# One load for the second row block of a weight matrix, in a kernel whose weight loads are issued from one queue

## The chip, the core and the metric

The kernel runs on one core of a Trainium2 chip. The metric is the device time in microseconds of one execution. Results of a pair come from the same chip in alternation. The profile shows one execution of each kernel; its span, from the first to the last instruction, is some 1.3 us shorter than that execution's time.

## The reference

Two branches work on the same input `x` of 2048 tokens by 640 features (bf16) and are mixed by a gate for each token:

```python
g = sigmoid((x * gate_w).sum(-1, keepdims=True))
a = state_space(x)                       # a linear recurrence over the 2048 tokens, 640 complex states
b = gelu(x @ w1 + b1) @ w2 + b2          # w1: 640 x 1728, w2: 1728 x 640
out = g * a + (1 - g) * b
```

What matters is the beginning: `x @ w1`. Its contraction runs over 640 features, five row blocks of 128 rows of `w1`.

## The kernel before

The kernel is written as operations with priorities. A list scheduler in the program, fed with guessed durations, fixes their order on each engine at build time. All loads that matter here are issued by the SP engine, in order of `prio` (cut, with `KN` = 2 filled in):

```python
WSPLIT = {1: 6, 3: 6}                    # row blocks of W1 whose first 1024 columns come in two loads

def w1load(k, eng, prio):
    edges = [0] + ([WSPLIT[k] * 128] if k in WSPLIT else []) + [FW]          # FW = 1024
    for i, (f0, f1) in enumerate(zip(edges, edges[1:])):
        load(f"w1_{k}{i}", eng, f"l_w1{k}{i}", W1sb[:, k, f0:f1],
             B_w1[k * 128:(k + 1) * 128, f0:f1], [("w1", k, i)], prio=prio + 0.1 * i, lat=2.6)

def w1tok(k, jf):                        # which of the loads a matmul has to wait for
    return ("w1", k, int(jf >= WSPLIT.get(k, NW)))

load("xna", "sp", ...)                   # 512 tokens, first 256 features
w1load(0, "sp", 1)
w1load(1, "sp", 1.3)
xtrans(0, range(2, 3), 1.6, 0.8)         # transpose while loading: input features 256 to 383
w1load(2, "sp", 2)
xtrans(0, range(3, 4), 3, 0.8)
w1load(3, "sp", 4)
xtrans(0, range(4, 5), 4.5, 0.8)
w1load(4, "sp", 5)
... # the other columns of W1, the state-space matrices, the rest
```

TensorE starts with matmuls on constants, which need no data, then transposes the first 256 features of `x` (`f_xt`, line 427, eight instructions), VectorE copies the results out of PSUM (line 433, four copies), and the first stage of the product follows (`m1_first`, line 640). It goes through seven of the eight output banks for row block 0 before it touches row block 1 (the eighth follows just before row block 1 needs it), so that loads can arrive while it works:

```python
steps = [(0, 0, 0), (0, 1, 0), (0, 0, 1), (0, 1, 1)] + [(k, jf, None) for k, jf in seq if k or jf > 1]
# ... one matmul each: 4 of 256 columns and 5 of 512 with row block 0,
#     then row block 1 (its last two steps are (0, 7), (1, 7)), then 2, 3, 4
```

The matmul that first reads row block 1 is thus TensorE's tenth in this stage. I call it **the tenth matmul** below.

Of the kernel before, what the change touches and what calls it, by code (L numbers as in the profile page):

```python
# [184 lines left out]
def bass_gated_mix__ssm_conv_s5__dense_activation_gelu__prompt_kernel(  # L185
# [40 lines left out]
    with ExitStack() as es:  # L226
# [127 lines left out]
            load_T(f"xT{q}_{ks[0]}", f"l_xT{q}_{ks[0]}", [(xT[q][:, ks[0]:ks[-1] + 1, :], x2[q * 512:(q + 1) * 512, ks[0] * 128:(ks[-1] + 1) * 128])],  # L354
                   [("xT", q, k) for k in ks], prio, dur)

        WSPLIT = {1: 6, 3: 6}

        def w1load(k, eng, prio):
            edges = [0] + ([WSPLIT[k] * 128] if k in WSPLIT else []) + [FW]  # L360
            for i, (f0, f1) in enumerate(zip(edges, edges[1:])):
                load(f"w1_{k}{i}", eng, f"l_w1{k}{i}", W1sb[:, k, f0:f1], B_w1[k * 128:(k + 1) * 128, f0:f1], [("w1", k, i)], prio=prio + 0.1 * i, lat=2.6)

        def w1tok(k, jf):
            return ("w1", k, int(jf >= WSPLIT.get(k, NW)))

# [727 lines left out]
```

## Time and profile before

| kernel before | value |
|---|---|
| time, median of the 3 runs given | 212.67 us (212.47 to 213.09) |
| span of the profiled run | 212.1 us |
| TensorE busy | 98% of the span |
| first matmul of `m1_first` | 5.25 us |
| the tenth matmul | 7.16 us |
| last matmul done | 210.15 us |

How to read it: TensorE is the bound, and a load can only matter where TensorE waits for it. So the profile has to be asked what TensorE waits for, and how long before its first use each load has landed (in the trace the semaphore of each of these loads has 16 increments, and the last is taken as the landing).

### The profile page before, as it was taken

What the parts mean: (1) busy time and instruction counts of PE and PEld (TensorE: products, weight loads), DVE (VectorE), ACT (ScalarE), POOL (GpSimd) and SP (SyncE); (2) the same over time, 40 slices, a digit from 0 to 9 for tenths busy, and PEclk for the clock granted to TensorE, in tenths of its full rate; (3) what the DMA queues carried; (4) which work ended last, traced back from release to release, by engine and by line L of the source; (5) the groups of instructions that cost most, each with busy time, mean ns of one, the idle gap of its engine ahead of it and who ended that gap; (6) DMA issues with size and microseconds to landing.
All of it is one profiled execution on the core that took longest, in us unless ns stands there. A gap on an engine that the chain in (4) does not pass through costs nothing.

```text
span 212.1 us, 2737 instructions
## 1 busy us (share of the span) xinstructions
PE 208.0 (98%) x1088; PEld 104.9 (49%) x1102; DVE 190.1 (90%) x240; ACT 103.0 (49%) x177; POOL 4.2 (2%) x12
## 2 busy tenths in 40 slices
PE   7999999999999999999999999999999999999996
PEld 3444444444564444444464444444446444567775
DVE  2399999999999999999999999899999999499744
ACT  2389556677960353556681063455660027623330
POOL 1000000030000000000000000000010000000000
DMA  5999999999600010075274000004742000005251
GB/s 163 202 279 135 207 171 198 380 222 162 185 12 3 0 49 0 0 85 111 54 59 114 3 0 0 0 2 115 96 96 117 0 3 0 0 0 104 68 140 63
DMA packets 48808, 19.08 MB, mean 90 GB/s; under 512 B 41500, under 2 KB 47772, under 8 KB 48796
## 3 DMA queue, kind: packets, MB, share of 16 engines
q1 hardware_dynamic: 47136, 17.59, 39.7%
q0 software_dynamic: 1600, 1.32, 4.5%
q8 instruction: 8, 0.13, 0.4%
q14 instruction: 4, 0.03, 0.1%
q10 hardware_dynamic: 60, 0.01, 0.0%
HBM read 8.41 MB, written 2.63 MB: 52 GB/s over the span
## 4 chain that ended last, share of the span: by engine, by line
PE 96%; DMA 2%; issue 1%; SPq 0%; DVE 0%
PE ps L662 22%; PE ps L705 20%; PE ps L929 20%; PE ps L978 15%; PE ps L792 7%; PE ps L841 5%; PE ps L640 4%; DMA W1sb<-in_B_w_dram 2%; PE ps L683 1%; PE ps L940 1%; PE ps L806 0%; SPq L333 0%; DVE W1sb L875 0%; PE ps L446 0%
## 5 line engine op out<-in xcount | busy, mean ns | idle before, releaser
L662 PE MATMUL ps<-xT,W1sb 128*128 128x512 bf16 x215 | 47.5, 379 | 0.3
L745 DVE TENSOR_TENSOR_SCAN W<-atab,V 128x1280 bf16<-128x1280 f32 x16 | 44.3, 2812 | 0.3
L705 PE MATMUL ps<-xT,BT 128*128 128x512 bf16 x196 | 43.1, 379 | 0.3 <-issue 0.2
L929 PE MATMUL ps<-Gl,W2sb 128*128 128x512 bf16 (+1 forms) x230 | 42.5, 343 | 0.2
L669 ACT ACTIVATE Gl<-ps,cols 128x512 bf16<-128x512 f32 x44 | 29.9, 694 | 15.5 <-PE ps L662 15.5
L662 PEld LDWEIGHTS ps<-xT,W1sb 128*128 128x128 bf16 x220 | 21.6, 98 | 25.9
L978 PE MATMUL ps<-Hb,CT 128*128 128x512 bf16 x150 | 32.9, 379 | 0.0
L929 PEld LDWEIGHTS ps<-Gl,W2sb 128*128 128x128 bf16 x234 | 22.9, 98 | 19.3
L705 PEld LDWEIGHTS ps<-xT,BT 128*128 128x128 bf16 x200 | 19.5, 98 | 23.7 <-ACT Gt L691 0.4
L714 ACT ACTIVATE U<-ps 128x512 bf16<-128x512 f32 x40 | 23.6, 599 | 14.6 <-PE ps L705 14.5
L947 ACT ACTIVATE E1T<-ps,cols 128x512 bf16<-128x512 f32 (+1 forms) x18 | 9.5, 624 | 36.0 <-PE ps L940 36.0
L978 PEld LDWEIGHTS ps<-Hb,CT 128*128 128x128 bf16 x150 | 14.5, 98 | 17.9 <-DVE V L496 0.6
L986 ACT ACTIVATE E2T<-ps 128x512 bf16<-128x512 f32 x15 | 9.1, 604 | 13.6 <-PE ps L978 13.6
L792 PE MATMUL ps<-W2sb,Gl 128*128 128x320 bf16 x104 | 14.8, 299 | 0.0
L615 DVE SCALAR_TENSOR_TENSOR trf<-xn,gwb 128x640 bf16<-128x640 bf16 x16 | 13.2, 823 | 0.4
L496 DVE TENSOR_TENSOR V<-V,W 128x1280 bf16<-128x1280 bf16 x16 | 12.5, 822 | 0.3
L496 DVE TENSOR_TENSOR Hb<-Hb,V 128x1280 bf16<-128x1280 bf16 x16 | 12.5, 822 | 0.3
L496 DVE TENSOR_TENSOR V<-mr,U 128x2560 bf16<-128x2560 bf16 x8 | 11.9, 1492 | 0.3
L792 PEld LDWEIGHTS ps<-W2sb,Gl 128*128 128x128 bf16 x104 | 10.1, 98 | 4.3 <-issue 0.3
L496 DVE TENSOR_TENSOR Hb<-c,W 128x2560 bf16<-128x2560 bf16 x8 | 11.9, 1491 | 0.2
L496 DVE TENSOR_TENSOR W<-mi,U 128x2560 bf16<-128x2560 bf16 x8 | 11.9, 1484 | 0.0
L496 DVE TENSOR_TENSOR V<-s,W 128x2560 bf16<-128x2560 bf16 x8 | 11.9, 1484 | 0.0
(91 smaller groups left out, 150.8 us busy)
## 6 DMA issues: line engine op xcount, KB each, us to landing
W2sb<-in_B_w_dram SPq DMA_DIRECT2D x1, 2080.0 KB, 8.9
out_dram<-xn SPq DMA_DIRECT2D x3, 640.0 KB, 4.8
xn<-in_A_x_dram POOLq DMA_DIRECT2D x2, 640.0 KB, 7.3
W1sb<-in_B_w_dram SPq DMA_DIRECT2D x3, 256.0 KB, 3.7
trf<-grow SPq DMA_DIRECT2D x3, 256.0 KB, 5.3
xn<-in_A_x_dram SPq DMA_DIRECT2D x1, 640.0 KB, 7.7
W1sb<-in_B_w_dram SPq DMA_DIRECT2D x1, 480.0 KB, 4.6
out_dram<-W1sb SPq DMA_DIRECT2D x3, 160.0 KB, 1.8
```

The source lines that it names most:

```text
L496: return inc("dve", nc.vector.tensor_tensor(out=o, in0=a, in1=b, op=o_))
L615: t = inc("dve", nc.vector.scalar_tensor_tensor(out=scr[:, :], in0=xn[q % 2][:, c, :], scalar=1.0, in1=gwb[:, :], op0=ALU.mult, op1=ALU.mu ...
L662: t = nc.tensor.matmul(PS[bank][:, :], W1sb[:, k, jf * 128:(jf + 1) * 128], xT[q][:, k, :], start=(k == 0), stop=(k == KD - 1))
L669: return inc("act", nc.scalar.activation(Gl[q % 2][:, jf, :], PS[bank][:, :], ACT.Gelu_apprx_tanh, bias=b1col[:, jf:jf + 1]))
L705: t = nc.tensor.matmul(PS[bank][:, :], BT[:, ci, kd, k * 128:(k + 1) * 128], xT[q][:, kd, :], start=(kd == 0), stop=(kd == KD - 1))
L714: return inc("act", nc.scalar.activation(dst, src, ACT.Copy, scale=1.0 if ci == 0 else -1.0))
L745: t = inc("dve", nc.vector.tensor_tensor_scan(out=g[:, ci, :], data0=a, data1=v[:, ci, :], initial=0.0, op0=ALU.mult, op1=ALU.add))
L792: t = nc.tensor.matmul(PS[bank][:, 0:HALF], Gl[q % 2][:, jf, t4 * 128:(t4 + 1) * 128], W2sb[:, jf, cols], start=False, stop=False, skip_gr ...
L841: t = nc.tensor.matmul(PS[bank][:, 0:n], H[b % NHB][:, ci, k, s * 128:(s + 1) * 128], CT[:, ci, k, cols], start=(i == 0), stop=(i == 2 * K ...
L929: t = nc.tensor.matmul(PS[bank][:, 0:t1 - t0], W2sb[:, jf, d * 128:(d + 1) * 128], Gl[q % 2][:, jf, t0:t1], start=(jf == 0), stop=False)
L947: return inc("act", nc.scalar.activation(E1T[:, d, t0:t1], PS[bank][:, 0:t1 - t0], ACT.Identity, bias=cols2[:, 0, d:d + 1]))
L978: t = nc.tensor.matmul(PS[bank][:, :].rearrange("p (s t) -> p s t", s=2), CT[:, ci, k, d * 128:(d + 1) * 128], Hb[:, 2 * (q % 2):2 * (q % ...
```

## The change

The intent is one DMA issue less on SP, and rows of 2 KB instead of 1.5 KB and 0.5 KB. The transposes of the state-space matrices stay cut in pieces of 512 and 128 rows. The whole diff:

```diff
-        WSPLIT = {1: 6, 3: 6}
+        WSPLIT = {3: 6}
```

With it, `w1tok` makes every matmul on row block 1 wait for the one load.

## The prediction

> **What bounds the kernel now.** I read the page first, the chain that ended last in order of time second, then who waited for whom on TensorE, and last the DMA queue (SP's issues and their landings) in the opening microseconds, because the change touches one load issued there. The page's busy shares, and its chain by engine:
>
> ```profile
> PE 208.0 (98%) x1088; PEld 104.9 (49%) x1102; DVE 190.1 (90%) x240; ACT 103.0 (49%) x177; POOL 4.2 (2%) x12
> ...
> PE 96%; DMA 2%; issue 1%; SPq 0%; DVE 0%
> ```
>
> The busy share alone would not prove that TensorE sets the end, since 98% may hide idle time between modelled matmul ends; the chain proves it: 96% of the span is TensorE following itself, and the only DMA in it has 2%. The chain in order of time (start us, us, what) tells where that DMA stands:
>
> ```profile
> 0.74 0.46 SPq L333
> 1.21 0.06 issue
> 1.26 3.85 DMA W1sb<-in_B_w_dram
> 5.12 0.14 issue
> 5.25 2.94 PE ps L640 x13
> 8.19 0.06 PE ps L446
> 8.25 4.32 PE ps L640 x20
> 12.56 0.05 issue
> 12.62 1.89 PE ps L640 x8
> 14.51 5.40 PE ps L662 x25
> ...
> 210.15 0.02 issue
> 210.17 0.35 DVE W1sb L875
> ```
>
> The reader is to see that the span has three parts: up to 5.25 us the first load of W1 (row block 0) must land; from 5.25 to 210.15 TensorE runs without a break longer than 0.16 us; then about 2 us of a last VectorE operation and its store. So a change can move the time only by moving 5.25, by putting a gap into the middle, or by lengthening the tail. TensorE's waits in the whole kernel confirm that no other load is waited for (engine line waited for: us in total, times, longest):
>
> ```profile
> PE ps L415 <- PEq L1079: 0.8, 1, 0.8
> PE ps L640 <- DMA W1sb<-in_B_w_dram: 0.5, 1, 0.5
> PE ps L705 <- issue: 0.2, 1, 0.2
> ```
>
> The one 0.5 us wait for W1 is that for row block 0. SP's queue in the opening (start us, us occupied):
>
> ```profile
> 0.74 0.46 SPq L333 DMA_DIRECT2D xn<-in_A_x_dram  x1
> 1.26 1.61 SPq L333 DMA_DIRECT2D W1sb<-in_B_w_dram  x3
> 2.92 1.20 SPq L340 DMA_TRANSPOSE xT<-in_A_x_dram  x1
> 4.17 0.58 SPq L333 DMA_DIRECT2D W1sb<-in_B_w_dram  x1
> 4.79 1.13 SPq L340 DMA_TRANSPOSE xT<-in_A_x_dram  x1
> ```
>
> Three W1 issues stand back to back: row block 0 (issued at 1.26), then row block 1's first 768 columns (1.80) and its last 256 (2.45). SP waits for nothing there, so each item's place depends only on what is issued before it.
>
> [...]row block 0's count being full at 5.12, row block 1's two pieces at 5.58 and 6.06. [...]The trace has 16 increments for each of these loads; of row block 0's, fifteen came by 4.28 us and the last at 5.12, so one late engine of sixteen decides. [...]The packet records show 27 ns for a 512 B packet, 65 ns for 1536 B and 84 ns for 2048 B (the common values).
>
> **The change, part by part.** In words: the table of split loads loses the entry for row block 1, so its 1024 columns (128 rows of 2 KB, 256 KB) arrive in one load instead of 192 KB and 64 KB. Row block 3 stays split, the transposes of the state-space matrices are as before ("still"), no compute operation is touched.
>
> 1. Removed: one issue on SP. It occupied 0.43 us, and the next item started at 2.92 against 2.45, so everything behind it on SP moves forward by 2.921 - 2.445 = 0.48 us at most, until SP first waits for compute. Those are the input transposes, row blocks 2 to 4, the rest of W1 and all later loads. It helps only if one of them is waited for on the chain; none is.
>
> 2. Removed: 128 small packets. Per row, 65 + 27 = 92 ns become 84 ns; over 128 rows and 16 engines that is 128 x 8 / 16 = 64 ns of DMA time. The load should have 128 packets fewer, so 48808 becomes about 48680 (an estimate, as counts vary by a few).
>
> 3. Moved: the first 768 columns' data now count as there only when the whole block is. The load is issued at the same 1.80 us, and its data are complete at worst about when the second piece's were, 6.06, and by step 1's shorter issue rather 5.6 to 6.0. Who needs it first? By single starts in the trace, row block 0's nine matmuls (four of 256 columns, five of 512) start from 5.25 to 6.95, and the first one with row block 1 at 7.16. The margin was 7.16 - 5.58 = 1.58 us and becomes 7.16 - 6.06 = 1.10 us in the worst case. Columns 768 on are first used at 8.51, with a margin of 2.45 us. So the coarser wait costs nothing.
>
> 4. Moved, margins behind it. Row block 2 lands at 7.87 and its input transpose at 6.69, needed at 9.16; row block 3's pieces land at 9.79 and 10.04, needed at 10.89 and 12.18; row block 4 at 11.78, needed at 12.62; W1's remaining columns at 13.49, needed at 14.34. The tightest are 0.84 and 0.85 us. They grow by up to the 0.48 us of step 1, or by less where the DMA engines are full: from 5.25 to 14.34 their share reads 0.97 to 1.20, so many bytes of slack are not there, and earlier issue gives less than earlier landing.
>
> 5. Removed: one semaphore wait on TensorE before the first matmul with the second piece. It was long satisfied; the starts around it are 8.299, 8.514, 8.730, the ordinary pitch of 0.216 us. Saved: nothing visible, well under 0.05 us.
>
> 6. The start, 5.25 us. Row block 0 is issued before the change's place, with the same bytes ahead of it. Its landing should stay, except for chance in the one late engine.
>
> Sum on the path: 0 from 1 to 4, 0 to -0.05 from 5, 0 plus chance from 6. The 0.48 us on SP and 0.06 us on the DMA engines are real but lie beside 204.9 us of unbroken TensorE work. From the median 212.67 I take 212.6.
>
> **The rivals.**
> - *A new wait at row block 1.* If the single load landed over 1.1 us later than the old second piece, TensorE would stop before its tenth matmul. For it: one late engine of sixteen carries the whole load, as row block 0's did by 0.84 us. Against it: even that lateness on top of 6.06 gives 6.90, still before 7.16. If it did happen, 0.1 to 0.5 us would be lost: up to 213.1.
> - *The start moves.* The queue behind row block 0 is 0.48 us earlier, so the first input transpose with its many 256 B packets (first seen between 4.5 and 5.0 us) overlaps row block 0's late tail, and its last engine could finish later; or the tail could be luckier. For it: after those packets the trace has 2048 B packets of 400 to 600 ns instead of 84. Against it: [...]the late packets belong to row block 2. Worth plus or minus 0.3 us at most; VectorE's input copies end at 5.06 anyway, so the start has at most some 0.2 us to gain without them.
> - *Gain in full.* If SP's issue were the bound, 0.48 us would come off: 212.2. The chain has SP with 0.46 us before the first load only, which does not move, so I hold this unlikely.
> - *Another order of instructions.* The kernel orders its operations by a list scheduler with guessed durations; one load less could let it choose differently. Its choices in the kernel before follow priority, with the few exceptions waiting for compute and none for a load, so I expect the same order. A different one could cost or gain about 1 us.
>
> **Range and chances.** The three times before lie between 212.47 and 213.09, a spread of 0.62 us from nothing but repetition. My expected change is below 0.1 us, so the range is that spread widened by the start's 0.3 us: 212.1 to 213.2. Faster or slower by 2% means 4.25 us, nearly ten times the only quantity that the change frees; both need something none of the views shows, 0.01 each.
>
> **What would show it.** Steps 1 and 2: SP's second W1 group reads two loads instead of three, the first transpose is issued at about 2.44 instead of 2.92, packets are about 128 fewer. Step 3: row block 1 lands between 5.5 and 6.2, and TensorE's waits still name W1 only once. Step 4: row blocks 2 to 4 land up to 0.48 us earlier and nobody's start follows. Step 6: TensorE's long run starts at 5.25 within 0.3 us and lasts 204.9 within 0.1. I am wrong if a second wait for W1 appears, if the run's length changes by over 0.2 us, or if the order of matmuls differs.

The sum stays 0 from steps 1 to 4, 0 to -0.05 us from 5 and 0 plus chance from 6, so 212.6 us from the median of 212.67. Where the prediction and the expectations speak of a late or last engine, the trace shows a late last semaphore increment (row block 0's fifteenth at 4.28 us, its sixteenth at 5.12); that it comes from one DMA engine is the author's reading, as the trace does not name the engine.

## The result, and the profile after

| | runs | median, us | lowest to highest, us |
|---|---|---|---|
| kernel before | 6 | 212.80 | 212.47 to 213.19 |
| changed kernel | 6 | 213.09 | 212.42 to 213.41 |

The ratio is 1.0008 with a 95% interval of 0.9988 to 1.0029: the same time. Ratios here are the mean time of one kernel's runs over that of the other's in the same rounds, so not quite the ratio of the medians. Experiment 6 gives a measure of the noise: there the kernel before was timed against itself, and its two medians differ by 0.35 us, more than the 0.29 us here.

On TensorE, VectorE, ScalarE and GpSimd the programs have the same instructions in the same order; SP has one load less. (The first profile of the kernel before lacks 14 of its 1102 matmul records; its second profile has them all.)

SP's queue of the changed kernel (start us, us occupied) answers to the queue shown in the prediction:

```profile
0.74 0.46 SPq L333 DMA_DIRECT2D xn<-in_A_x_dram  x1
1.27 1.14 SPq L333 DMA_DIRECT2D W1sb<-in_B_w_dram  x2
2.45 1.20 SPq L340 DMA_TRANSPOSE xT<-in_A_x_dram  x1
3.70 0.64 SPq L333 DMA_DIRECT2D W1sb<-in_B_w_dram  x1
4.39 1.13 SPq L340 DMA_TRANSPOSE xT<-in_A_x_dram  x1
```

Two loads of W1 stand where three were, and the first input transpose is issued at 2.45 us instead of 2.92. The page's line of DMA packets, first of the kernel before, then of the changed one:

```profile
DMA packets 48808, 19.08 MB, mean 90 GB/s; under 512 B 41500, under 2 KB 47772, under 8 KB 48796
```

```profile
DMA packets 48664, 19.08 MB, mean 90 GB/s; under 512 B 41484, under 2 KB 47500, under 8 KB 48652
```

There are 144 fewer packets: 128 rows of data and 16 small packets (4 bytes each, the only ones under 512 B that went), as many as the removed load has semaphore increments. Under 2 KB 272 are gone, 128 + 128 + 16, because the rows of both old pieces counted there and the new 2 KB rows don't. The diff is thus wholly visible in the trace.

The chain that ended last of the changed kernel, in order of time:

```profile
0.78 2.93 PE ps L415 x7
3.71 0.03 issue
3.74 0.37 PE ps L427 x2
4.11 0.02 issue
4.13 0.70 DVE xT L433 x3
4.83 0.05 issue
4.88 2.54 PE ps L640 x13
7.42 0.06 PE ps L446
7.48 6.26 PE ps L640 x29
...
209.38 0.02 issue
209.40 0.35 DVE W1sb L875
```

Held against the chain in the prediction, two things differ, and the experiments will show that neither needs the change. The stage starts at 4.88 us instead of 5.25, and its first thirteen matmuls take 2.54 us instead of 2.94. Together this makes the span 0.8 us shorter, while the timed runs show no gain at all. A reader who compared just these two profiles would find a gain that isn't there. What these two differences are had to be found out first.

TensorE's waits in the changed kernel:

```profile
PE ps L415 <- PEq L1079: 0.8, 1, 0.8
PE ps L640 <- DVE xT L433: 0.5, 1, 0.5
```

No load is named, row block 1 least of all.

**The start.** The chain, like the second of these lines, puts the start down to VectorE's copies. But the first matmul needs only the first copy, done at 4.42 us (4.13 plus 0.29, by the single records). Row block 0's load had all 16 increments at 4.75 us, and the matmul started 0.13 us later. In the kernel before, the same load was complete at 5.12 us and the matmul started 0.13 us later as well. The profile puts a wait for several semaphores down to what came last; here VectorE's third copy, which this matmul does not need, ended at 4.83 us, just behind the landing, and was named in its place. Two of the experiments below have the same distance, 4.60 to 4.74 and 4.63 to 4.77 us. So in these four profiles the landing of row block 0 set the start, and that depends on the last of its 16 increments: fifteen had come by 4.28 us before (the last at 5.12) and by 4.57 after (the last at 4.75).

**The pace.** In the kernel before, the eight small transposes start 0.107 us apart and the first matmuls of 256 columns 0.213 us apart; in the changed kernel's profile the transposes are 0.056 us apart from the fourth on, and those matmuls 0.108. So TensorE began this stage at half pace in one execution and at full pace in the other. Its seven matmuls on constants (512 columns) start at 0.78 us and then mostly 0.427 us apart in both profiles, half the pace of the 0.216 us seen later; in the profiles without a long wait before it, full pace came between about 3.7 and 6.5 us, 2.9 to 5.8 us after that first matmul. The view of the transposes' line tells it too. Here it is for two executions of the changed kernel, the profile above and that of experiment 5 (least, median and most ns of one, as the profile models its end; first and last start):

```profile
L427 PE MATMUL ps<-ident,xn x8: 219/219/289, 3.7 to 4.2; 128*128 128x128 bf16 x8
```

```profile
L427 PE MATMUL ps<-ident,xn x8: 288/314/314, 3.7 to 4.4; 128*128 128x128 bf16 x8
```

The mean granted clock reads 1.000 for these executions, so it does not tell of this; the distance between starts does.

### The profile page after: what moved, and what is told of

Its sections match the earlier page's. It is cut to its first block, busy times and chain, and to the rows that moved or that the text cites. A ratio compares the mean times of both kernels' runs of the same rounds, so it can differ in the third digit from the quotient of the medians.

```text
span 211.3 us, 2750 instructions
## 1 busy us (share of the span) xinstructions
PE 208.1 (98%) x1102; PEld 104.4 (49%) x1102; DVE 190.1 (90%) x240; ACT 102.9 (49%) x177; POOL 4.2 (2%) x12
## 2 busy tenths in 40 slices
DMA packets 48664, 19.08 MB, mean 90 GB/s; under 512 B 41484, under 2 KB 47500, under 8 KB 48652
## 4 chain that ended last, share of the span: by engine, by line
PE 98%; DVE 0%; issue 0%
PE ps L662 22%; PE ps L705 20%; PE ps L929 20%; PE ps L978 15%; PE ps L792 7%; PE ps L841 5%; PE ps L640 4%; PE ps L415 1%; PE ps L683 1%; PE ps L940 1%; DVE xT L433 0%; PE ps L806 0%; PE ps L427 0%; DVE W1sb L875 0%; PE ps L446 0%
## 5 line engine op out<-in xcount | busy, mean ns | idle before, releaser
L662 PE MATMUL ps<-xT,W1sb 128*128 128x512 bf16 x220 | 48.1, 379 | 0.0
L705 PE MATMUL ps<-xT,BT 128*128 128x512 bf16 x200 | 43.8, 379 | 0.0
```

Of the source, the lines that this page charges most:

```text
L662: t = nc.tensor.matmul(PS[bank][:, :], W1sb[:, k, jf * 128:(jf + 1) * 128], xT[q][:, k, :], start=(k == 0), stop=(k == KD - 1))
L705: t = nc.tensor.matmul(PS[bank][:, :], BT[:, ci, kd, k * 128:(k + 1) * 128], xT[q][:, kd, :], start=(kd == 0), stop=(kd == KD - 1))
```

## The experiments

Eight runs in two sets, every one with a profile, and timed against the kernel before in five rounds. The theory was: the loads lie beside TensorE's work; the change is free because row block 1 lands before the tenth matmul, with or without the split; and the spread of the times comes from the start and the pace. The rivals: SP's issue time counts in full; the margin plays no part; the whole load has a small cost.

### 1. Row block 3 whole as well

```diff
-        WSPLIT = {3: 6}
+        WSPLIT = {}
```

> Row block 3 is loaded whole as well, so one more issue leaves SP. Theory (loads lie beside TensorE's work, the time is the start of its long run plus some 204.5 us): the transposes and loads behind it are issued another 0.48 us earlier, the time stays within 0.4 us of the changed kernel's, 212.4 to 213.4. Rival (SP's issue time is on the path): another 0.48 us off, about 212.2.

Measured: median 213.04 us (212.72 to 213.44), ratio to before 0.9998 (0.9964 to 1.0033). The third input transpose was issued at 6.19 us instead of 6.66, so another 0.47 us was freed on SP, and the time did not fall. TensorE waits for no load of W1. The interval of this run alone reaches down to 0.9964, some 0.8 us, and would not exclude the rival, but no run was below 212.72 us. The interval of the main result does exclude it: its lower end, 0.9988, leaves 0.26 us of the 0.48 us that the change freed. With the table of all profiles further down, the rival that would have it at 212.2 us falls: SP's issue time is not on the path.

### 2. Row block 1 behind the first input transpose

The guessed latency is changed with the priority only to keep the scheduler's order of matmuls, which is the same as in the changed kernel.

```diff
-... prio=prio + 0.1 * i, lat=2.6)
+... prio=prio + 0.1 * i, lat=1.0 if k == 1 else 2.6)
-        w1load(1, "sp", 1.3)
+        w1load(1, "sp", 1.7)
```

> Row block 1's single load is issued behind the first input transpose, some 1.2 us later than in the changed kernel. The profile of the changed kernel had it landed at 6.04 us and needed at 6.39, that of the kernel before needed it at 7.16. Theory (the change was free because of that margin, which is only 0.35 to 1.1 us): it lands at about 7.0 to 7.2, TensorE's waits name W1 before the tenth matmul, and the time rises by 0.1 to 0.8 us, to about 213.3. Rival (the margin is well over 1 us, or the block's landing never matters): no such wait, time as before.

Measured: median 213.00 us (212.79 to 213.45), ratio 0.9999 (0.9965 to 1.0033). The load landed at 6.63 us, earlier than the 7.0 to 7.2 expected, and TensorE's tenth matmul started at 6.67, 0.64 us after the ninth instead of 0.22: a stall of 0.42 us (the profile's lines below count 0.3 us, from the modelled end of the ninth). TensorE's waits in this kernel, without the one at its very beginning:

```profile
PE ps L640 <- DVE xT L433: 0.3, 1, 0.3
PE ps L640 <- DMA W1sb<-in_B_w_dram: 0.3, 1, 0.3
```

The second line is the new wait. The expected rise of the time is not resolved: the profiled execution was at full pace from its first transpose on, and gave back by the wait what others lose by pace. So the wait of the theory came, and the time of the rival. The six times say no more: their lowest is 212.79 us, but experiment 1, without such a wait, has 212.72 in the same rounds.

### 3. Row block 1 behind the transpose and row block 2

The same edit with a priority of 2.5.

> Row block 1's single load behind the first input transpose and row block 2's load, some 0.65 us later again. Theory: it lands at about 7.5 to 7.9, TensorE waits before its tenth matmul by about 0.4 to 1.4 us, and the time rises by about 0.4 to 1.4 us, 0.5 more than with the load behind the transpose alone. Rival (landing does not matter): time as before.

Measured: median 213.79 us (213.61 to 214.10), ratio 1.0034 (0.9997 to 1.0072). The load landed at 7.52 us and the tenth matmul started at 7.57. The chain of this kernel:

```profile
3.80 3.72 DMA W1sb<-in_B_w_dram
7.52 0.05 issue
7.57 1.04 PE ps L640 x4
```

The chain no longer begins with row block 0: the load of row block 1, issued at 3.80, carries it, and TensorE continues 0.05 us after it has landed. Its interval against before just holds 1. Against experiment 2 in the same rounds the mean rises by 0.8 us (213.80 against 213.04), for 0.9 us of later landing, and all six runs are longer than any of that experiment's. The rival that landing does not matter falls; the margin is what made the change free.

### 4. Row blocks 0 and 1 exchanged

```diff
-        w1load(1, "sp", 1.3)
+        w1load(1, "sp", 0.5)
```

> Row block 1's load is issued ahead of row block 0's: the same issues and bytes, exchanged in order. Theory (row block 0's landing sets the start of the long run): it lands 0.5 to 1.2 us later, at about 5.5 to 6.0, the run starts as much later and the time rises by 0.5 to 1.2 us, to about 213.7. Rival (the start is set by the input's transposes and VectorE copies, as the chain of the changed kernel has it, or only the sum of bytes counts): start 4.9 to 5.2, time as before.

Measured: median 215.50 us (215.21 to 215.84; 4 runs), ratio 1.0115 (1.0072 to 1.0157). Row block 0 landed at 6.03 us and the stage started at 6.17, again 0.14 us later, as the theory had it. The medians differ by 2.7 us, over twice the most that was expected (2.5 us by the ratio). The windows of this kernel (window; its length, then busy us and instructions of each engine; granted clock, DMA share, GB/s) show the rest:

```profile
4.40:6.10 1.70, 0.00 (x0) 0.00 (x0) 0.52 (x3) 0.53 (x1) 0.00 (x0) 1.00 1.16 187
6.17:7.00 0.83, 0.83 (x6) 0.58 (x7) 0.00 (x0) 0.00 (x0) 0.00 (x0) 0.99 1.00 262
7.00:10.00 3.00, 3.00 (x8) 1.06 (x7) 0.00 (x0) 0.00 (x0) 0.00 (x0) 0.50 0.96 204
10.20:14.00 3.80, 3.80 (x20) 1.73 (x19) 3.15 (x9) 2.96 (x6) 0.00 (x0) 0.97 1.12 280
```

TensorE is idle in the first window; that is the wait of 1.8 us. TensorE then works for 0.8 us at full pace and falls to a granted clock of 0.50 for three microseconds, in which it gets through eight matmuls instead of some fourteen. Its matmuls of 512 columns start 0.427 us apart there instead of 0.216. Against the changed kernel's profile the span is 3.0 us longer: the stage starts 1.3 us later, and eight matmuls with an excess of 0.21 us make about 1.7 us more. That the wait brought about the fall of the clock was not tested, and the fall was seen in this one execution only: the three other runs, 215.21 to 215.84 us, have a recorded clock of 1.000, and what slowed them is not seen. The same 256 KB, exchanged with its neighbour in the queue, costs about 1%, where the change itself costs nothing that shows.

### 5. The changed kernel once more

> The changed kernel once more. Theory (the change lies wholly beside TensorE's work, and two chances make the spread: when row block 0 has landed on its last DMA engine, and when TensorE's first matmuls leave half pace): ratio 1.000 with an interval that holds 1; start between 4.7 and 5.3 us, long run 204.3 to 205.1 us, row block 1 landed at about 6.05 and no wait for it. Rival (a cost of the whole load too small to see so far): ratio 1.001 or more with an interval above 1, or a wait for W1 at the tenth matmul.

Measured: median 212.89 us (212.30 to 213.23), ratio 0.9992 (0.9947 to 1.0038; the interval is wide because one of the eleven runs of before took 215.49 us). The stage started at 4.53 us, earlier than the 4.7 to 5.3 expected, and row block 1 landed at 6.05, with no wait for it. The run from the first matmul to the last took 205.4 us, a little over what was expected, because its first matmuls went at half pace until 6.53 us. No small cost of the whole load shows; by the times alone this interval would hide 0.8 us and that of the main result 0.6 us, so that there is none rests on the table of the profiles.

### 6. The kernel before against itself

> The kernel before against itself, as a measure of the noise and a second look at its start. Theory: ratio within 0.2% of 1; row block 1's first piece landed at about 5.6 and its second at about 6.05; start and half pace differ from the first profile by chance, so that the span moves by up to 0.8 us with no change at all. Rival (the two profiles before and after differed by 0.8 us because of the change): the span is 212.1 again within 0.2.

Measured: median 212.98 us (212.75 to 213.43), ratio 1.0006 (0.9965 to 1.0047). The stage started at 4.57 us, 0.68 us earlier than in the first profile of the same kernel, and its run took 205.2 us instead of 204.9; the span was 211.8 us. Row block 1's second piece landed at 5.85 us, not at the 6.05 expected, so landings move by 0.2 us as well. The start of the chain, as in experiment 5, is now TensorE alone:

```profile
0.78 2.93 PE ps L415 x7
3.71 0.04 issue
3.75 1.04 PE ps L427 x8
4.78 3.06 PE ps L640 x13
```

Here row block 0 had landed at 4.40 us and the transposes, at half pace, took 1.04 us and set the start (4.78 is the modelled end of the last transpose, 4.57 the recorded start of the next matmul). The rival, that the 0.8 us between the first two profiles came of the change, asked for a span of 212.1 within 0.2 again; at 211.8 it misses that by 0.1 only. What rules it out is the table further down, in which start and pace account for all of the difference, and differ by nearly as much between two executions of one kernel.

### 7. Row block 1 in four loads

```diff
-        WSPLIT = {3: 6}
+        WSPLIT = {1: (2, 4, 6), 3: (6,)}
-            edges = [0] + ([WSPLIT[k] * 128] if k in WSPLIT else []) + [FW]
+            edges = [0] + [e * 128 for e in WSPLIT.get(k, ())] + [FW]
-            return ("w1", k, int(jf >= WSPLIT.get(k, NW)))
+            return ("w1", k, sum(jf >= e for e in WSPLIT.get(k, ())))
```

(The step of the priorities is halved as well, so that all four stay ahead of the transpose.)

> Row block 1 in four loads of 256 columns: three issues more on SP than in the changed kernel, so everything behind moves back by some 1.4 us. Theory (an issue is free only while the margins behind it last, and these were 0.8 us for row block 2 and 0.3 to 0.9 us for row block 4): the first piece lands by 5.2 us, but the later input columns and row blocks come about 1 us later and TensorE waits two or three times, 0.3 to 1.0 us in sum, so about 213.4. Rival (DMA engines are the limit, not SP's issue): landings of row blocks 2 to 4 stay within 0.3 us, no wait, time as before.

Measured: median 213.34 us (213.23 to 213.66), ratio 1.0022 (0.9981 to 1.0062, with the same slow run of before in it). Against experiment 5 in the same rounds the mean rises by 0.5 us (213.38 against 212.84), against experiment 6 by 0.3 us; that is little more than the noise, and the waits in the profile show the cause better. The first piece landed at 5.23 us, but row block 2 only at 8.38 (changed kernel: 7.56) and row block 4 at 12.10 (11.59). TensorE waits three times: the single starts are 0.61, 0.49 and 0.55 us apart at 8.51, 12.23 and 19.68 us, where 0.216 is usual, 1.0 us in sum. Two of the waits in the profile's words:

```profile
PE ps L640 <- DMA W1sb<-in_B_w_dram: 0.2, 1, 0.2
PE ps L705 <- DMA BT<-in_A_B_re_dram: 0.2, 1, 0.2
```

The second is for a transpose of a state-space matrix, issued long behind the four pieces. The pieces also bring 384 more data packets than the whole load; by the prediction's 27 and 84 ns a packet that is, as an estimate, 0.2 us of time on 16 engines, beside 1.5 us of later issue for row block 2 (5.18 against 3.70 us). The two were not separated, but the larger is the issue. An issue occupied SP for 0.43 to 0.64 us for a plain load of W1 and 1.1 to 1.3 us for a transposing load of 512 x 128, small beside the 3.5 to 5.3 us from issue to landing of W1's loads in the kernel before; but three more added up to 1.0 us of waits. So issue slots on SP are not free as such. They were free in the change because the margins behind them held.

### 8. Row block 0 from ScalarE's queue

```diff
-        w1load(0, "sp", 1)
+        w1load(0, "act", -150)
```

> Row block 0 issued from ScalarE's queue as its first item, beside the input load on SP, and all of SP's later loads 0.53 us earlier. Theory (row block 0's landing sets the start): it lands at 4.2 to 4.5 us, the start is then set by the input's transposes and first copy, 4.5 to 4.7, and the time falls by 0.1 to 0.4 us, to about 212.5. Rival ([...]the input lands later by what row block 0 gains): input landed at 4.0 or later instead of 3.7, start unchanged or later, time as before or 0.3 us more.

Measured: median 214.04 us (213.13 to 215.38), ratio 1.0056 (1.0004 to 1.0108). The rival was right that the input would land later, though the time rose by more than the 0.3 us that it allowed: row block 0 landed at 4.19 us, but the input, loaded beside it, at 4.85 instead of 3.69. What the two loads share is not shown by the trace. The longest of TensorE's waits:

```profile
PE ps L427 <- DMA xn<-in_A_x_dram: 1.2, 1, 1.2
```

The times fall into two groups, three at 213.13 to 213.21 and three at 214.88 to 215.38. The profile is of the slow group (its execution took 214.90 us), and its matmuls stay at half pace until 8.62 us. This was the one attempt at a version that beats both kernels. It doesn't, and the experiments point to no other.

### What all ten profiles have in common

All times in us. "Last" is the end of the last matmul in the chain; the tenth is the first matmul that reads row block 1, and "landed" is the time at which that block's load (in the split kernels its first piece) was complete.

| kernel | first | tenth | landed | last | last - tenth |
|---|---|---|---|---|---|
| before | 5.25 | 7.16 | 5.58 | 210.15 | 202.99 |
| before again | 4.57 | 6.82 | 5.60 | 209.80 | 202.98 |
| changed | 4.88 | 6.39 | 6.04 | 209.38 | 202.99 |
| changed again | 4.53 | 6.96 | 6.05 | 209.95 | 202.99 |
| no split | 4.71 | 6.66 | 6.08 | 209.64 | 202.98 |
| behind one | 4.74 | 6.67 | 6.63 | 209.67 | 203.00 |
| behind two | 4.77 | 7.57 | 7.52 | 210.57 | 203.00 |
| ScalarE's queue | 5.72 | 8.62 | 5.62 | 211.61 | 202.99 |
| four pieces | 4.59 | 6.12 | 5.23 | 210.11 | 203.99 |
| exchanged | 6.17 | 8.35 | 4.27 | 212.35 | 204.00 |

From the tenth matmul on, eight of the ten executions take 202.98 to 203.00 us, whatever was done to the loads. The two others have their reason in this stretch: the three waits of experiment 7 (1.0 us), and the matmuls that were still at half pace behind the tenth in experiment 4. So neither the free 0.48 us on SP nor the saved packets reach the end. Everything that differs between before and changed lies ahead of the tenth matmul: between the first two profiles 7.16 - 6.39 = 0.77 us, which is 0.37 us of start and 0.40 us of pace, against 0.8 us between their spans. And two executions of one and the same kernel differ there by nearly as much: 6.39 and 6.96 for the changed one, 0.57 us.

## Why the prediction was right

**The time.** Predicted 212.6 us in a range of 212.1 to 213.2, measured 213.09 (213.04 and 212.89 in the experiments that share the idea or repeat it): within the range and within 2%, as was given a chance of 0.98. It was a near thing: the median is 0.11 us below the upper end of the range, and two of the six runs, at 213.41, are above it. As the kernel before against itself shows, the noise alone moves a median by more than that, so the place within the range is luck; that the change would be worth nothing is not.

**Step 1, the issue removed from SP,** was right in size (0.47 us, from 2.92 to 2.45) and in worth. Experiment 1 freed as much again for nothing, and experiment 7 showed the condition on which it is free.

**Step 2, the packets.** Predicted about 48680, measured 48664; the 16 packets of 4 bytes that went with the removed load were forgotten. By the packet times in the prediction a packet of 512 B moves 19 bytes per ns (512 in 27 ns) and one of 2048 B 24 (in 84 ns), so the short rows were somewhat slower for each byte here. Nothing of it reaches the path.

**Step 3, the coarser wait,** came to the right end with a wrong margin. The landing came out at the worst case, not better: 6.04, 6.05 and 6.08 us in three profiles (the first is 1.80 for the issue plus 4.24 to landing), for "6.06" at worst and "rather 5.6 to 6.0". The shorter issue brought it nothing. The need was off by more. I took 7.16 us from one profile and called the margin of 1.10 us the worst case; but that profile had a late start and half pace, and so a late tenth matmul. In the changed kernel's own profile the margin was 6.39 - 6.04 = 0.35 us. As an estimate from these rows, an execution with the earliest start seen, 4.53, and the fastest pace seen for nine matmuls, 1.51 us, would need row block 1 at 6.04, just when it lands. The change is free, but an execution with the luckiest start and pace would have nothing left of the margin. Experiment 2 shows what the next 0.6 us does: a stall of 0.42 us.

**Step 4, the margins behind,** was right only in that no wait came. Row blocks 2 and 4 landed at 7.56 and 11.59 us instead of 7.87 and 11.78, earlier by less than 0.48 us, as was argued from the DMA share of 0.97 to 1.20 (that the share is the reason was an estimate); but row block 3's two pieces came at 9.03 and 9.27 instead of 9.79 and 10.04, earlier by more than the issue moved, and the kernel before had them at 9.45 and 9.64 in its second profile. So single landings vary by 0.3 to 0.4 us without a change. And the margins did not grow. They too were read from the late profile: in the changed kernel's own, row block 4 was needed at 11.85 us, a margin of 0.26 instead of 0.84 us and the smallest of all, smaller than row block 1's. It moves as much without the change (0.84 and 0.36 us in the two profiles of the kernel before, 0.26 and 1.55 in those of the changed kernel), but it shows how little lay behind "no wait".

**Step 5, one wait less on TensorE:** nothing visible, as said; the matmuls on row block 1's last columns start 0.216 us apart in both kernels.

**Step 6, the start,** was wrong as a statement of size. "Within 0.3 us" of 5.25 and a run that "lasts 204.9 within 0.1" both failed: the starts of the two kernels in four profiles lie from 4.53 to 5.25 us, the run from 204.5 to 205.4. By my own test, a run's length changed by over 0.2 us, the mechanism would have been refuted. The test was bad, not the mechanism: I knew of the late last increment but not of the pace, and a single profile does not show that a pace is half if one has nothing to compare it with. The prediction also gave the start at most 0.2 us to gain, because VectorE's copies end at 5.06; but the first matmul needs only the first copy, which ended at 4.43, and the start came as early as 4.53. In the four profiles the starts spread by 0.72 us, the runs by 0.92 and the ends by 0.77, so the two chances cancel only in part.

**The rivals.** A new wait at row block 1 did not appear in any of the three profiles with the whole load in its place. Its dismissal was unsafe all the same: with a last increment as late as row block 0's (0.84 us) the load was put at 6.90 us, "still before 7.16", but the changed kernel's profile needed it at 6.39, so that no wait came is in part luck. The order of instructions did not change. That the start moves was true, but between executions of one kernel too (5.25 and 4.57, 4.88 and 4.53 us), and nothing shows that the change moved it. (The packets that this rival put at 400 to 600 ns are eleven of 306 to 764 in the records.)

What stays open: two of the 22 runs of the kernel before in the experiments took 215.16 and 215.49 us, and none of the twelve runs of the changed kernel did. They have no profile. They are as slow as the slow group of experiment 8, so half pace, as that group's profile has it until 8.62 us, would fit; but this was not seen, and two runs do not show a difference between the kernels.

## What to carry to other kernels

In these profiles a load beside the busy engine was worth its margin and nothing more (no wait with 0.35 us of it left, a stall of 0.42 us with the load landing 0.6 us later): first ask which load the bound engine waits for, then how long before its first use each of the others has landed. Read such a margin from several executions, since one profile gives one sample of start and pace; here the whole load's was 0.35, 0.58 and 0.91 us in three, where 1.10 was read from one profile as the worst case. To show that a change reaches nothing, pick an instruction behind it and compare the time from there to the end: 202.99 us in both kernels says more than two spans that differ by chance.
